# Block-sparse attention and a two-layer MoE in one kernel: V in three prepared layouts, the weight conversion in steps of its own, x in two rings of five

## The chip, the cores and the metric

One core of a Trainium2 chip runs the whole program. It has five engines with a queue of their own: TensorE (PE), VectorE (DVE), ScalarE (ACT), GpSimd (POOL) and SyncE (SP), which here issues every DMA. Each queue runs its instructions strictly in program order, and an instruction that has to wait holds up all that stand behind it. The metric is the device time of one execution in microseconds (us). Before the change it is 1017.01 us, the median of three runs (1015.11 to 1021.48).

## What is computed

```
# attention: batch 4, 8 heads, 768 positions, 64 per head, 24 blocks of 32
scores = (q @ k.T) / sqrt(64)
mask   = |block(i) - block(j)| <= 1, or block i or j is 0 or 23, or j in sampled_blocks[i] (3 per block)
attn   = softmax(where(mask, scores, -1e9));  x = (attn @ v) put together as [3072, 512]
# MoE layer: w_in [512, 2048], w_out [2048, 512]
h = x @ w_in
g = h where h >= 1, 0 where h <= -1, (h + 1)^2 / 4 between
out = g @ w_out
```

The weights arrive as 64-bit floats. The kernel turns them into 32-bit floats with integer operations, and each 32-bit number into a high and a low part, so that three fast matmul passes (high-high, high-low, low-high) give the wanted precision.

## The kernel before

**Attention** is done in pairs: a pair is one batch entry `b` (0 to 3) and two heads (`j`, 0 to 3). A pair goes through four rounds of query blocks: round 0 is the global blocks against all keys, rounds 1 to 3 take 6, 8 and 8 of the other 22 blocks. A round is a chain: `scores` (PE, line 298), `top` (row maxima, DVE, line 309), `expo` (ACT, lines 326 and 329), `turn` (transposes on PE, line 335), `turn_copy` (line 339, ACT or DVE), `values` (PE, line 353), `norm` (DVE, lines 376 to 380). After rounds 2 and 3 a half of `x` is transposed (`x_turn`), and stored as high and low part (`x_hi` on ACT, `x_lo` on DVE) in tile `xt`.

Three tiles hold the V rows of a pair. `vn` holds all rows. `va` holds in its four partition quarters, for each block, the block before it, the block itself, the block after it and block 0; `vb` holds the last block and the three sampled blocks. A sampled block is copied from `va` to `vb` on POOL (line 266) or read from memory by a DMA on SP (line 264); `V_SPW` says which of the three go by SP in the first batch entry, `V_SP` in the others. The sampled K columns go to `kg` (line 231), on POOL, and for `k in KD` on DVE in the first batch entry. A pair of the first batch entry is "wide": its rounds 0, 1 and 2 run before any MoE work and use all PSUM banks, and `TCOPYW` and the table `PW` hold for it. Its round 3 comes later, with `va`, `q` and `k` loaded again.

**The MoE layer** has eight stages, one for each half (384 tokens) of each batch entry. A stage goes over 16 slices `fi` of the hidden dimension: `l1` (lines 472 to 474), the activation (ACT and DVE), `l2` (lines 500 to 502). In the first stage w_out is converted on the way, two slices at a time, and kept in memory (`w_keep`); later stages load it back (`w_load`).

**Conversion** (`convert`, lines 156 to 186) comes sixteen times: eight for w_in (conversions 0 to 7, of which 4 to 7 are for the second half of its columns, wanted from slice 8 on) and eight for w_out (8 to 15). One is: `load` of tile `raw` (two DMAs of 512 KB, line 163), `bits` (an Abs on ACT at line 170, then four DVE operations, lines 171 to 176, into tile `cva`), and `split` (a cast to the high part on ACT, line 75 by way of a helper, and a subtraction on DVE, line 182). `raw` and `cva` have one buffer each, so a load can't start until the `bits` of the conversion before are done.

**What sets the order.** Every step is put into a list with a planned time (`at`), worked out from the tables `P`, `PW`, `PD` and from `TP0`, `CONV` and the like. The list is sorted, and the steps are written into the program in that order. Nothing waits for a planned time: it decides only who stands ahead of whom in each queue. On SP each DMA uses one of eight completion counters in turn, so a DMA also waits until the one eight places ahead of it has landed.

The later batch entries are interleaved with the MoE stages. `xt` has six buffers for each of its two halves (`XBUFS`), and `X2`, `X3` shift the second half of the pairs 2 and 3 to a later place.

Of the kernel before, what the change touches and what calls it, by code (L numbers as in the profile page):

```python
# [27 lines left out]
VROWS = S + BLK  # L28
# [13 lines left out]
def body(ctx, tc, qk_t, v_ext, sampled_blocks, moe_w_in, moe_w_out, near, ident, out):  # L42
# [7 lines left out]
    xp = pool("xp", XBUFS)  # L50
# [19 lines left out]
    def f(ap):  # L70
        return ap.bitcast(F32)
# [70 lines left out]
    def plan_conversions():  # L142
        last = 1e9
        todo = []
        for t, *rest in sorted(conv, key=lambda x: -x[0]):
            last = min(t, last - P["cd"])
            todo.append((last, *rest))
        prev = -1e9
        for t, load, bits, split, parts in todo[::-1]:
# [6 lines left out]
    def convert(t, src, parts):  # L156

        st = {}

        def load():  # L160
            st["raw"] = cv.tile([128, 1024, 2], I32, name="raw", bufs=RAWB)
            for k in range(2):
                Q_RAW.dma_start(out=st["raw"][:, k * 512:(k + 1) * 512],
                                in_=src[k].bitcast(I32).rearrange("p (c w) -> p c w", w=2))

        def bits():
            raw = st["raw"]
            lo32, hi32 = raw[:, :, 0], raw[:, :, 1]
            a = st["a"] = cv.tile([128, 1024], I32, name="cva", bufs=CVAB)
            nc.scalar.activation(out=f(a), in_=f(hi32), func=AF.Abs)  # L170
# [8 lines left out]
        def split(cs, dst, done):  # L179
            hi, lo = dst()  # L180
            rounded(CH, hi, f(st["a"][:, cs]))
            nc.vector.tensor_tensor(out=lo, in0=f(st["a"][:, cs]), in1=f(hi), op=ALU.subtract)
            if done:
                done()

        conv.append((t, load, bits, split, parts))


# [12 lines left out]
    def pair(b, j, s, q, wide, rounds=(0, 1, 2, 3)):  # L201
# [44 lines left out]
        def gather_v(r):  # L246
            vb = st["vb", r] = gat.tile([128, 8, VROW], F32, name="vb", bufs=VBUFS)
            for k0, i0, n in runs(r):
                c = 1 if i0 + n == NB - 1 else 0
                Q_V.dma_start(out=vb[0:32, k0:k0 + n - c], in_=rows(S - BLK, BLK, n - c, 0))  # L250
                if c:
                    Q_V.dma_start(out=vb[0:32, k0 + n - 1:k0 + n], in_=rows(S, BLK, 1, 0))

        def gather_v_sampled(r, engine):
            vb = st["vb", r]
            for k0, i0, n in runs(r):
                for k in range(n):
                    for a in range(NR):
# [128 lines left out]
        def x_hi(hf):  # L387
            x = xt[b, j, hf] = xp.tile([128, 2, HALF], F32R, name=f"xt{hf}")
# [11 lines left out]
        for k, r in enumerate(rounds):  # L400
# [25 lines left out]
            if r >= 2:  # L426
                y = y + G["va"] + G["no"] + (0 if b == 0 or r == 2 else (0, 0, X2, X3)[j])
# [4 lines left out]
                else:  # L432
                    wanted.append((y + G["xt"], steps, r - 2))
# [15 lines left out]
    def moe(t0, p, b, hf, first):  # L449
# [41 lines left out]
        def g_lo(fi):  # L491
            gl = g["gl", fi] = mt.tile([128, HALF], F32R, name="gl", bufs=2)
            (nc.gpsimd if first and fi % 4 in GL1 else nc.vector).tensor_tensor(out=gl, in0=g["r", fi], in1=f(g["gh", fi]), op=ALU.subtract)  # L493
# [95 lines left out]
_INS = ["qk_t", "v_ext", "sampled_blocks", "moe_w_in", "moe_w_out"]  # L589
# [15 lines left out]
def _rows(_np, a):  # L605
# [3 lines left out]
    return _np.concatenate([a, _np.zeros((B, NP, BLK, VROW), _np.float32)], axis=2)  # L609
# [30 lines left out]
```

## Time and profile before

| | us |
|---|---|
| median of three runs | 1017.01 |
| the profiled execution, its own time | 1015.81 |
| its span, first to last instruction | 1014.0 |
| PE busy in it | 837.8 |
| DVE, ACT, POOL busy | 435.8, 411.8, 387.0 |

In the views below a row of a timeline gives the start, the length, the engine and what it did ("x12" is twelve instructions merged), and in brackets how long the engine had stood idle and who released it. "SPq" is the queue of SP: its rows are DMA issues, and their length includes what the issue waits for. A row of waits gives the total of a kind of wait, how often, and the longest. The granted clock (PEclk) is a share of the full TensorE clock of 2.4 GHz; 0.5 is the lower level of 1.2 GHz.

### The profile page before, as it was taken

The page shows a single profiled execution, that of the slowest core. Times are in us where ns is not written, and L with a number is a line of the kernel's source. Part 1 is how long each engine was busy: PE and PEld are TensorE (multiplying, and loading weights), DVE is VectorE, ACT ScalarE, POOL GpSimd, SP SyncE. Part 2 cuts the span into 40 slices and gives each one's busy share as a digit, 9 for nine tenths or more (in the row PEclk, how much of TensorE's full clock was granted, in tenths as well). Part 3 has the DMA queues.
Part 4 walks back from the last instruction along what each step waited for, and adds up shares of the span by engine and source line. Part 5 has one row for each costly group of instructions (what it writes and reads, how often), then busy time and mean ns, then how long its engine had stood idle before and what let it go on. Part 6 is the DMA issues. An engine that isn't in the chain of part 4 may idle for free.

```text
span 1014.0 us, 34082 instructions
## 1 busy us (share of the span) xinstructions
PE 837.8 (83%) x12000; PEld 691.2 (68%) x12000; DVE 435.8 (43%) x1013; ACT 411.8 (41%) x812; POOL 387.0 (38%) x1564
## 2 busy tenths in 40 slices
PE   2532634775778899899999999999999999999997
PEld 1321423654666677777888887887777777899996
DVE  6555753553546343444444434344443343322222
ACT  1432432433343443445444544354444343433433
POOL 2011133558265656645454545555453630000000
PEclk9857657997798999999999999999999999999999
DMA  8467658998574674637474757465645732433432
GB/s 187 103 175 165 132 148 173 240 229 221 174 192 118 178 184 131 138 110 188 145 168 138 183 154 167 139 177 147 173 122 170 163 103 96 151 129 125 156 125 94
DMA packets 137599, 157.54 MB, mean 155 GB/s; under 512 B 13779, under 2 KB 108756, under 8 KB 137428
## 3 DMA queue, kind: packets, MB, share of 16 engines
q1 hardware_dynamic: 137428, 155.35, 57.6%
q8 instruction: 96, 1.57, 0.7%
q14 instruction: 75, 0.61, 0.2%
HBM read 140.61 MB, written 14.68 MB: 153 GB/s over the span
## 4 chain that ended last, share of the span: by engine, by line
PE 63%; DVE 13%; DMA 8%; ACT 7%; issue 4%; SPq 3%; DVEq 1%; ACTq 0%
PE oa L500 8%; PE h L472 8%; PE oa L501 7%; PE oa L502 7%; PE h L474 6%; PE h L473 6%; PE o L353 6%; PE s L298 6%; PE t L335 5%; DMA raw<-in_moe_w_out_dram 3%; DVE m L309 3%; DMA raw<-in_moe_w_in_dram 3%; ACT p L329 2%; DVE pt L339 2%; SPq L264 2%
## 5 line engine op out<-in xcount | busy, mean ns | idle before, releaser
L231 POOL COPY kg<-k 128x32 f32 x912 | 178.0, 227 | 283.8 <-PE s L298 195.1
L266 POOL COPY vb<-va 32x130 f32 x648 | 208.8, 326 | 162.5 <-DMA va<-in_v_ext_dram 102.4
L472 PE MATMUL h<-xt,wi 128*128 128x384 f32 x448 | 164.9, 368 | 38.1 <-DVE r L484 26.7
L500 PE MATMUL oa<-w,gh 128*128 128x512 f32 x384 | 163.8, 427 | 0.4 <-ACT gh L75 0.3
L474 PE MATMUL h<-xt,wi 128*128 128x384 f32 x448 | 154.1, 344 | 0.0
L473 PE MATMUL h<-xt,wi 128*128 128x384 f32 x448 | 154.0, 344 | 0.0
L502 PE MATMUL oa<-w,gl 128*128 128x512 f32 x384 | 152.8, 398 | 0.0
L501 PE MATMUL oa<-w,gh 128*128 128x512 f32 x384 | 152.2, 396 | 0.0
L478 ACT ACTIVATE r<-h,half_c 128x384 f32<-128x384 f32 x112 | 65.3, 583 | 164.5 <-PE h L474 164.0
L484 DVE SCALAR_TENSOR_TENSOR r<-r,h 128x384 f32<-128x384 f32 x112 | 61.7, 551 | 146.5 <-ACT r L481 146.3
L472 PEld LDWEIGHTS h<-xt,wi 128*128 128x128 f32 x448 | 86.9, 194 | 52.2 <-DVE r L484 31.5
L335 PE MATMUL t<-idf,p 128*128 128x128 f32 x464 | 78.2, 293 | 42.1 <-ACT p L326 18.5
L335 PEld LDWEIGHTS t<-idf,p 128*128 128x128 f32 x464 | 54.5, 147 | 70.3 <-ACT p L326 27.0
L75 ACT CAST gh<-r 128x384 fp32r<-128x384 f32 x128 | 65.7, 514 | 89.3 <-DVE r L484 88.8
L493 DVE TENSOR_TENSOR gl<-r,gh 128x384 fp32r<-128x384 f32 x128 | 72.3, 565 | 60.1 <-ACT gh L75 59.8
L329 ACT ACTIVATE p<-s,m 128x256 f32<-128x256 f32 x176 | 71.8, 473 | 62.4 <-DVE m L321 53.0
L473 PEld LDWEIGHTS h<-xt,wi 128*128 128x128 f32 x448 | 87.2, 195 | 4.6 <-issue 1.4
L474 PEld LDWEIGHTS h<-xt,wi 128*128 128x128 f32 x448 | 86.5, 193 | 0.0
L500 PEld LDWEIGHTS oa<-w,gh 128*128 128x128 f32 x384 | 72.9, 190 | 17.0 <-issue 3.9
L502 PEld LDWEIGHTS oa<-w,gl 128*128 128x128 f32 x384 | 72.6, 189 | 16.7 <-DVE gl L493 0.3
L298 PE MATMUL s<-k,q 64*32 64x96 f32 (+2 forms) x3376 | 72.8, 267 | 11.6 <-DMA q<-in_qk_t_dram 6.2
L501 PEld LDWEIGHTS oa<-w,gh 128*128 128x128 f32 x384 | 73.3, 191 | 6.6
(87 smaller groups left out, 1132.3 us busy)
## 6 DMA issues: line engine op xcount, KB each, us to landing
w<-wo_dram SPq DMA_DIRECT2D x112, 512.0 KB, 3.4
va<-in_v_ext_dram SPq DMA_DIRECT2D x40, 357.5 KB, 8.2
raw<-in_moe_w_in_dram SPq DMA_DIRECT2D x16, 512.0 KB, 6.2
raw<-in_moe_w_out_dram SPq DMA_DIRECT2D x16, 512.0 KB, 8.4
wo_dram<-w SPq DMA_DIRECT2D x16, 512.0 KB, 5.7
va<-in_v_ext_dram SPq DMA_DIRECT2D x20, 406.2 KB, 5.9
k<-in_qk_t_dram SPq DMA_DIRECT2D x20, 384.0 KB, 5.0
q<-in_qk_t_dram SPq DMA_DIRECT2D x20, 384.0 KB, 4.2
```

What stands on the lines that cost most here:

```text
L231: eng.tensor_copy(out=kg[:, k0 + k, 32 * a:32 * a + 32], in_=kt[:, bass.ds(field(v, a, NB - 1) * BLK, BLK)])
L266: nc.gpsimd.tensor_copy(out=dst, in_=st["va"][32:64, bass.ds(v, 1)].rearrange("p a d -> p (a d)"))
L298: nc.tensor.matmul(out=st["s", r, e][32 * w:32 * w + 32, 256 * g + c0:256 * g + c1], lhsT=st["q"][es, i * BLK:(i + 1) * BLK], rhs=rhs, sta ...
L329: nc.scalar.activation(out=p[:, 256 * g:256 * g + 256], in_=st["s", r, e][:, 256 * g:256 * g + 256], func=AF.Exp, bias=st["m", r][:, e, g: ...
L335: nc.tensor.transpose(out=t[:, c * 128:(c + 1) * 128], in_=st["p", r, e][:, c * 128:(c + 1) * 128], identity=idf)
L472: nc.tensor.matmul(out=hv, lhsT=wi[:, j, 0, fs], rhs=x[:, 0], start=(j == 0), stop=False)
L473: nc.tensor.matmul(out=hv, lhsT=wi[:, j, 0, fs], rhs=x[:, 1], start=False, stop=False)
L474: nc.tensor.matmul(out=hv, lhsT=wi[:, j, 1, fs], rhs=x[:, 0], start=False, stop=(j == NP - 1))
L493: (nc.gpsimd if first and fi % 4 in GL1 else nc.vector).tensor_tensor(out=gl, in0=g["r", fi], in1=f(g["gh", fi]), op=ALU.subtract)
L500: nc.tensor.matmul(out=o, lhsT=gh[:, ts], rhs=w[:, 0], start=(fi == 0), stop=False)
L501: nc.tensor.matmul(out=o, lhsT=gh[:, ts], rhs=w[:, 1], start=False, stop=False)
L502: nc.tensor.matmul(out=o, lhsT=gl[:, ts], rhs=w[:, 0], start=False, stop=(fi == NF - 1))
```

## The change

V comes in three arrays that the host lays out beforehand: `v_rows` for `vn`, `v_near` for `va` (each partition's 25 blocks in one run of 13,000 bytes, with zeros where nothing belongs), and `v_last` for the last block in `vb`. Each of `vn` and `va` becomes one DMA over 128 partitions, and the last block one DMA a round.

```
-            Q_V.dma_start(out=va[32:64], in_=rows(0, BLK, NB + 1, BLK))
-            Q_V.dma_start(out=va[0:32, 1:NB - 1], in_=rows(0, BLK, NI, BLK))
-            Q_V.dma_start(out=va[64:96, 1:NB - 1], in_=rows(2 * BLK, BLK, NI, BLK))
-            Q_V.dma_start(out=va[96:128, 2:NB - 1], in_=rows(0, BLK, NI - 1, 0))
-            Q_V.dma_start(out=va[96:128, 1:2], in_=rows(S, BLK, 1, 0))
+            Q_V.dma_start(out=va, in_=v_near[b, j])
...
-            for k0, i0, n in runs(r):
-                c = 1 if i0 + n == NB - 1 else 0
-                Q_V.dma_start(out=vb[0:32, k0:k0 + n - c], in_=rows(S - BLK, BLK, n - c, 0))
-                if c:
-                    Q_V.dma_start(out=vb[0:32, k0 + n - 1:k0 + n], in_=rows(S, BLK, 1, 0))
+            k = 3 if r == 1 else 0
+            Q_V.dma_start(out=vb[0:32, 0:total], in_=v_last[b, j, :, k:k + total])
```

`bits` is cut into `size` (the Abs) and `bits` (the DVE operations), `split` into `high` and `low`, each with a planned time of its own (`cb`, `cz`), and `cva` has two buffers. All tables are new. In the first batch entry fewer sampled K columns go to DVE and fewer sampled V blocks to SP (both to POOL), and one more `turn_copy` goes from ACT to DVE. `xt` has two rings of five, and a store into it is planned no earlier than about the end of the stage that frees its buffer.

```
-            at(t, bits)
+            at(t, size)
+            at(t + P["cb"], bits)
             for later, *part in parts:
-                at(t + P["cs"] + later, split, *part)
+                at(t + P["cs"] + later, high, *part)
+                at(t + P["cs"] + P["cz"] + later, low, *part)
...
+                    old = (b * NP + j - XB[r - 2]) // NP
+                    free = NP * TP0 + DELAY + (old * 2 + r - 1) * 1.5 * TPM - 4.0 if old >= 0 else 0
+                    wanted.append((max(y + G["xt"], free), steps, r - 2))
...
-KD = (0, 1, 2, 4)
+KD = (0,)
-V_SPW = (0, 1)
+V_SPW = (0,)
-RAWB, CVAB = 1, 1
+RAWB, CVAB = 1, 2
-TCOPYW = (0, 1)
+TCOPYW = (0,)
-XBUFS = 6
+XB = (5, 5)
-CONV, CSTEP = 5.557, 8.518
-CONV1, CSTEP1 = 38.599, 8.708
+CONV, CSTEP = 5.244, 11.074
+CONV1, CSTEP1 = 47.887, 8.285
```

By the tables conversions 4 to 7 stood at the planned times 38.6, 47.3, 56.0 and 64.7 and stand at 47.9, 56.2, 64.5 and 72.7, where the first `l1` is planned at 81.1 before and 82.4 now; conversion 8 goes from 76.4 to 77.4.

In the queue of SP, this is what stood between the sampled blocks of the first pair and those of the second (`va`, `vn` and `vb` are the V tiles, `raw` the weights, `k` and `q` the next pair's inputs):

```order
L240 DMA va<-in_v_ext_dram 32x25x130
L241 DMA va<-in_v_ext_dram 32x22x130
L242 DMA va<-in_v_ext_dram 32x22x130
L243 DMA va<-in_v_ext_dram 32x21x130
L244 DMA va<-in_v_ext_dram 32x130
L163 DMA raw<-in_moe_w_in_dram 128x1024 x2
L207 DMA k<-in_qk_t_dram 128x768
L207 DMA q<-in_qk_t_dram 128x768
L211 DMA vn<-in_v_ext_dram 128x6x130
L250 DMA vb<-in_v_ext_dram 32x3x130
L250 DMA vb<-in_v_ext_dram 32x2x130
L252 DMA vb<-in_v_ext_dram 32x130
```

And this is what stands there in the changed kernel:

```order
L243 DMA va<-in_v_near_dram 128x3250
L214 DMA q<-in_qk_t_dram 128x768
L214 DMA k<-in_qk_t_dram 128x768
L218 DMA vn<-in_v_rows_dram 128x780
L165 DMA raw<-in_moe_w_in_dram 128x1024 x2
L249 DMA vb<-in_v_last_dram 32x780
```

Thirteen DMAs have become seven. In the stretch behind it the sampled blocks of rounds 1 and 2 of a wide pair were 12 and 16 DMAs and are 6 and 8, with one DMA for the last block ahead of the 16 where there were two.

In the queue of ACT, this stood where the last conversion of w_in passes into the first of w_out, just ahead of the first MoE stage (`L170` is the Abs of a conversion, `L75` the cast of one, `pt` a turn copy, `xt` the last half of x that the stage needs, `p` the exponentials of the first round 3):

```order
L329 ACTIVATE p<-oa_1885,m_1934 128x256 x2
L75 CAST wi<-cva 128x1024
L339 COPY pt<-h 128x512
L339 COPY pt<-t 128x512
L170 ACTIVATE cva<-raw 128x1024
L389 CAST xt_2153<-h 128x384
L329 ACTIVATE p<-s,m_2150 128x256 x4
L75 CAST w<-cva 128x512
```

In the changed kernel it is:

```order
L326 ACTIVATE p<-oa_1841,m_1890 128x256 x2
L170 ACTIVATE cva<-raw 128x1024
L336 COPY pt<-h 128x512
L170 ACTIVATE cva<-raw 128x1024
L74 CAST wi<-cva 128x1024
L386 CAST xt_2112<-h 128x384
L326 ACTIVATE p<-s,m_2115 128x256 x4
L74 CAST w<-cva 128x512
```

The Abs of conversion 7 now stands behind the last exponentials of the wide pairs (before, it stood ahead of them), and that of conversion 8 two places behind it, ahead of the cast of conversion 7 and of the last store to `xt`.

## Rows read from the trace of the kernel before

**Rows 1.** The page: the span.

```profile
span 1014.0 us, 34082 instructions
```

**Rows 2.** The windows view in four stretches: up to the first `l1`, up to the first output of the first MoE stage, up to about the end of the attention work, and the rest. Columns: length, busy time of PE, of its weight loads, of DVE, ACT and POOL (instructions in brackets), granted clock, busy share of the DMA engines, GB/s.

```profile
0.00:176.10 176.10, 69.69 (x1741) 50.60 (x1741) 99.80 (x299) 54.22 (x94) 33.03 (x129) 0.73 0.66 155
176.10:342.60 166.50, 125.05 (x1854) 101.47 (x1854) 85.50 (x158) 68.58 (x134) 98.20 (x354) 0.88 0.78 197
342.60:850.00 507.40, 485.24 (x7469) 398.22 (x7470) 205.46 (x474) 223.83 (x461) 255.76 (x1083) 1.00 0.56 151
850.00:1014.00 164.00, 157.81 (x939) 140.92 (x937) 45.05 (x83) 65.20 (x123) 0.00 (x0) 0.99 0.37 127
```

**Rows 3.** Marks of the stages: the timeline of PE with the round-0 scores of pairs 0, 1 and 3 (a group of 32 matmuls each), the view of line 472 with the first and last start of `l1`, and the timeline of SP with the first output.

```profile
6.21 1.96 PE L298 MATMUL s<-k,q 64*32 64x256 f32 x32 [6.21 <-DMA q<-in_qk_t_dram]
...
41.70 1.82 PE L298 MATMUL oa<-k,q 64*32 64x256 f32 x32
...
120.33 1.09 PE L298 MATMUL oa<-k,q 64*32 64x256 f32 x32
...
L472 PE MATMUL h<-xt,wi x448: 332/338/689, 176.1 to 999.1; 128*128 128x384 f32 x150
...
342.62 0.85 SPq L510 DMA_DIRECT2D out_dram<-ot  x2
```

**Rows 4.** The waits view from 0 to 157 us.

```profile
POOL vb L266 <- DMA va<-in_v_ext_dram: 90.7, 5, 31.8
ACT cva L170 <- DMA raw<-in_moe_w_in_dram: 37.0, 5, 13.7
DVE cva L171 <- ACT cva L170: 33.5, 6, 10.7
```

**Rows 5.** The timeline of SP from one load of conversion weights to the next but one, in the third pair.

```profile
86.92 0.83 SPq L163 DMA_DIRECT2D raw<-in_moe_w_in_dram  x2
...
91.01 2.23 SPq L250 DMA_DIRECT2D vb<-in_v_ext_dram  x2
...
94.07 9.73 SPq L264 DMA_DIRECT2D vb<-in_v_ext_dram  x12
103.91 0.83 SPq L163 DMA_DIRECT2D raw<-in_moe_w_in_dram  x2
104.84 0.85 SPq L250 DMA_DIRECT2D vb<-in_v_ext_dram  x2
105.96 10.74 SPq L264 DMA_DIRECT2D vb<-in_v_ext_dram  x16
116.80 0.36 SPq L240 DMA_DIRECT2D va<-in_v_ext_dram  x1
...
120.68 1.72 SPq L244 DMA_DIRECT2D va<-in_v_ext_dram  x1
122.51 0.82 SPq L163 DMA_DIRECT2D raw<-in_moe_w_in_dram  x2
```

**Rows 6.** The view of tile `raw`: the time from a DMA's issue to its landing over all 32 loads (least, median, most). Then single rows of the timelines of ACT and SP: the Abs of conversions 1, 8, 9 and 15, the two issues of the loads for conversions 9 and 10.

```profile
DMA to landing us min/median/max: 3.6/7.0/10.3
...
38.70 1.12 ACT L170 ACTIVATE cva<-raw 128x1024 f32<-128x1024 f32 x1 [2.31 <-DMA vb<-in_v_ext_dram]
...
169.27 1.12 ACT L170 ACTIVATE cva<-raw 128x1024 f32<-128x1024 f32 x1 [11.28 <-DMA raw<-in_moe_w_out_dram]
...
177.19 0.83 SPq L163 DMA_DIRECT2D raw<-in_moe_w_out_dram  x2
...
186.83 1.20 ACT L170 ACTIVATE cva<-raw 128x1024 f32<-128x1024 f32 x1 [0.76 <-DVE w L182]
...
192.06 1.21 SPq L163 DMA_DIRECT2D raw<-in_moe_w_out_dram  x2
...
307.58 1.13 ACT L170 ACTIVATE cva<-raw 128x1024 f32<-128x1024 f32 x1
```

**Rows 7.** The view by line and shape, whole span: busy time and mean ns of the Abs, of the four DVE operations of `bits`, of a turn copy on DVE and of a K copy on DVE.

```profile
L170 ACT ACTIVATE cva<-raw 128x1024 f32<-128x1024 f32 x16 | 18.2, 1138 | 72.3 <-DMA raw<-in_moe_w_in_dram 37.0 <-DMA raw<-in_moe_w_out_dram 29.7 <-DVE w L182 3.3
L171 DVE TENSOR_SCALAR cva<-cva 128x1024 f32<-128x1024 f32 x16 | 11.3, 708 | 66.2 <-ACT cva L170 66.2
L172 DVE TENSOR_SCALAR cva<-cva 128x1024 int32<-128x1024 int32 x16 | 11.2, 699 | 0.5
L174 DVE SCALAR_TENSOR_TENSOR cva<-raw,cva 128x1024 int32<-128x1024 int32 x16 | 19.6, 1228 | 0.5
L176 DVE SCALAR_TENSOR_TENSOR cva<-raw,cva 128x1024 int32<-128x1024 int32 x16 | 19.6, 1227 | 0.6
L339 DVE COPY pt<-t 128x512 f32<-128x512 f32 x52 | 35.9, 691 | 67.8 <-PE t L335 67.8
L231 DVE COPY kg<-k 128x32 f32 x144 | 24.4, 186 | 10.5 <-issue 6.8
```

**Rows 8.** The timeline of POOL: one round of K copies and two rounds of V copies in the first MoE stage.

```profile
175.25 5.01 POOL L231 COPY kg<-k 128x32 f32 x24 [11.07 <-DMA k<-in_qk_t_dram]
180.32 5.63 POOL L266 COPY vb<-va 32x130 f32 x16
...
201.50 8.83 POOL L266 COPY vb<-va 32x130 f32 x16 [1.87 <-DMA va<-in_v_ext_dram]
```

**Rows 9.** The waits view, whole span: the one wait of `l1` for a half of x.

```profile
PE h L472 <- DVE xt L393: 8.5, 1, 8.5
```

More of the change, by code (lines that the diff above doesn't have):

```diff
@@ L41, in body @@
 @with_exitstack
-def body(ctx, tc, qk_t, v_ext, sampled_blocks, moe_w_in, moe_w_out, near, ident, out):
+def body(ctx, tc, qk_t, v_rows, v_near, v_last, sampled_blocks, moe_w_in, moe_w_out, near, ident, out):
     nc = tc.nc
@@ L49, in body @@
     pr = pool("pr", 2)
-    xp = pool("xp", XBUFS)
+    xp = pool("xp", 1)
     mt = pool("mt", 2)
@@ L148, in plan_conversions @@
         prev = -1e9
-        for t, load, bits, split, parts in todo[::-1]:
+        for t, load, size, bits, high, low, parts in todo[::-1]:
             at(max(t - P["cl"], prev + 0.1), load)
             prev = t
-            at(t, bits)
+            at(t, size)
+            at(t + P["cb"], bits)
             for later, *part in parts:
-                at(t + P["cs"] + later, split, *part)
+                at(t + P["cs"] + later, high, *part)
+                at(t + P["cs"] + P["cz"] + later, low, *part)
     def convert(t, src, parts):
+        n = len(conv)
         st = {}
@@ L164, in load, with size @@
                                 in_=src[k].bitcast(I32).rearrange("p (c w) -> p c w", w=2))
+        def size():
+            a = st["a"] = cv.tile([128, 1024], I32, name="cva", bufs=CVAB)
+            nc.scalar.activation(out=f(a), in_=f(st["raw"][:, :, 1]), func=AF.Abs)
         def bits():
-            raw = st["raw"]
+            a, raw = st["a"], st["raw"]
             lo32, hi32 = raw[:, :, 0], raw[:, :, 1]
-            a = st["a"] = cv.tile([128, 1024], I32, name="cva", bufs=CVAB)
-            nc.scalar.activation(out=f(a), in_=f(hi32), func=AF.Abs)
             nc.vector.tensor_scalar(out=f(a), in0=f(a), scalar1=CLO, scalar2=CHI, op0=ALU.max, op1=ALU.min)
@@ L177, in bits, with high, low @@
                                            op0=ALU.logical_shift_right, op1=ALU.bitwise_or)
[L179 to L182, printed above, removed]
+        def high(cs, dst, done):
+            st[cs.start] = dst()
+            rounded(CH, st[cs.start][0], f(st["a"][:, cs]))
+        def low(cs, dst, done):
+            hi, lo = st[cs.start]
+            (nc.gpsimd if n in SUBP else nc.vector).tensor_tensor(out=lo, in0=f(st["a"][:, cs]), in1=f(hi), op=ALU.subtract)
             if done:
                 done()
-        conv.append((t, load, bits, split, parts))
+        conv.append((t, load, size, bits, high, low, parts))
     xt = {}
@@ L492, in g_lo @@
             gl = g["gl", fi] = mt.tile([128, HALF], F32R, name="gl", bufs=2)
-            (nc.gpsimd if first and fi % 4 in GL1 else nc.vector).tensor_tensor(out=gl, in0=g["r", fi], in1=f(g["gh", fi]), op=ALU.subtract)
+            (nc.gpsimd if first and fi in GL1 else nc.vector).tensor_tensor(out=gl, in0=g["r", fi], in1=f(g["gh", fi]), op=ALU.subtract)
         def l2(fi, t):
@@ L608, in _rows @@
     a = a.transpose(0, 1, 3, 2, 4).reshape(B, NP, S, VROW)
-    return _np.concatenate([a, _np.zeros((B, NP, BLK, VROW), _np.float32)], axis=2)
+    rows = a.reshape(B, NP, S // 128, 128, VROW).transpose(0, 1, 3, 2, 4)
+    blocks = a.reshape(B, NP, NB, BLK, VROW).transpose(0, 1, 3, 2, 4)
+    near = _np.zeros((B, NP, 4, BLK, NB + 1, VROW), _np.float32)
+    near[:, :, 0, :, 1:NB - 1] = blocks[:, :, :, 0:NB - 2]
+    near[:, :, 1, :, 0:NB] = blocks
+    near[:, :, 2, :, 1:NB - 1] = blocks[:, :, :, 2:NB]
+    near[:, :, 3, :, 2:NB - 1] = blocks[:, :, :, 0:1]
+    last = _np.zeros((B, NP, BLK, 9, VROW), _np.float32)
+    last[:, :, :, 0:8] = blocks[:, :, :, NB - 1:NB]
+    return rows, near.reshape(B, NP, 128, NB + 1, VROW), last
 def kernel(**inputs):
```

36 lines of the change are left out of this document (16 added, 20 removed).

## Prediction, made before the changed kernel ran

> **What bounds the kernel now.** I read the windows view first, by stages. The span is 1014.0 us [rows 1] and the execution took 1015.81, so 1.8 us lie outside it; the median of the runs is 1.2 above that execution. PE is busy for 69.7 of the first 176.1 us, for 125.1 of the next 166.5, for 485.2 of 507.4 and for 157.8 of the last 164.0 [rows 2]. Its idle time is therefore 106.4, 41.5, 22.2 and 6.2 us: 148 of 176 us lie ahead of 342.6. After that PE has work 96% of the time and the granted clock is 1.00 or 0.99; a change can win little there. So the question is what the first 342.6 us wait for.
>
> Next the marks and the timeline of SP. The wide pairs follow each other every (120.33 - 6.21) / 3 = 38.0 us, the first `l1` comes at 176.1 and the first output at 342.6 [rows 3]. In the third pair one turn of SP's queue, from the load at 86.92 to the next but one at 122.51, takes 35.6 us, about that pitch, and is full from end to end [rows 5]: 28 sampled blocks take 9.73 + 10.74 = 20.5 us (0.73 each), the five DMAs of `va` take from 116.80 to 122.40, which is 5.6 us. SP is the engine that the pairs go at.
>
> The waits say how that reaches the others: POOL stood 90.7 us for `va`, ACT 37.0 us in front of the Abs for `raw`, DVE 33.5 us for that Abs [rows 4]. The last two matter most, since exponentials, maxima and turn copies stand behind them in the same queues, and PE stands behind those. The conversions form one chain, because `raw` has one buffer: issue, landing, Abs, four DVE operations, next issue. Conversion 1 has its Abs at 38.70, conversion 8 at 169.27, conversion 15 at 307.58 [rows 6]: a pitch of 130.6 / 7 = 18.7 us, then of 138.3 / 7 = 19.8 us. The first `l1` follows conversion 8 by 6.8 us and the first output conversion 15 by 35.0 us [rows 3, 6]. So the first stage's end is 38.7 + 7 x 18.7 + 7 x 19.8 + 35.0 = 342.6, and the change is worth what it takes from these four terms.
>
> **SP, per wide pair.** Sampled blocks go from 28 DMAs to 14: 14 x 0.73 = 10.2 us instead of 20.5. `va` goes from five DMAs to one: about a fifth of 5.6, 1.1 us. The last blocks go from five DMAs to two. In the rows the first two took 2.23 and the two of round 2 0.85, so 1 us remains. Two loads of `raw` at 0.83 stay (1.7 us) [rows 5], and `q`, `k` and `vn` are three issues more, 1.2 us at the 0.41 that one of the two of `raw` took. The sum is 15.2 us instead of 35.6. SP stops being the bound as long as a pair takes more than that.
>
> **The conversion chain in the wide pairs.** What remains is the chain itself: 0.83 for two issues, the landing, 1.14 for the Abs and 0.71 + 0.70 + 1.23 + 1.23 = 3.86 for the DVE operations [rows 5, 7], so 5.8 us and the landing. A landing took 3.6 to 10.3 us, 7.0 in the middle [rows 6]. V's many small packets go, the bytes of the weights stay, so I take 6.7, near the median: a pitch of 12.5 us, or 25 us a pair. The high end is the longest landing, 16.1 us. The low end is set by DVE: it is busy 99.8 us in the first stretch [rows 2], loses 24 K copies of 0.186 a pair and gains three turn copies of 0.69 [rows 7], a net -2.4 us a pair, so about 90 us or 22.6 a pair, which is 11.3 us a conversion. I take 12.5: it lies 1.2 above what DVE can do without a wait.
>
> **The start.** The load of conversion 1 stood behind 12 sampled blocks and now behind 6 (4.4 us by 0.73), but the Abs stands behind the exponentials of round 2 in ACT's queue, and round 1 must now wait for twelve K and twelve V copies on POOL. I take 36 us for the Abs of conversion 1 instead of 38.7; bounds 33 and 38.7.
>
> **The first MoE stage.** The fastest turn of the chain there was 9.6 us from issue to Abs (177.19 to 186.83) and 5.2 us from Abs to the next issue (to 192.06), 14.9 in all [rows 6]; the mean was 19.8 because SP was in `va` or sampled blocks when `raw` came free, and because the DMA engines were full. The stretch moved 197 GB/s at a busy share of 0.78, while the last stretch, which has no V, moved 127 at 0.37 [rows 2]. At that second efficiency the same bytes need 197 / (127 / 0.37) = 0.57 of the time, 96 us, instead of 130. V is only a part of the bytes and the sampled blocks stay small, so between 96 and 130 I expect about 105 us of DMA work, in a shorter stage. That leaves the landing still loaded but not queued: I take 14.5 us, just under the fastest turn. The low end is PE: 125.05 us at a clock of 0.88 is 110 us of work at full clock, so conversion 8 to first output is not below 6.8 + 110 = 117 us, against 7 x 14.5 + 35 = 136.5. The high end is halfway from the fastest turn to the mean, 17.3.
>
> **What I cost at nothing.** The 24 K copies and 14 V copies a pair that go to POOL lie beside the chain. A round of POOL copies shows 0.209 us a K copy and 5.63 / 16 = 0.35 a V copy [rows 8], so 30 and 28 of them make 16.1 us of a pair's 25. Without that cover, if POOL reads at the slower of the two rounds shown (8.83 us, 0.55 each), it is 21.7 us, still below 25. The Trainium skill, SBUF — State Buffer, section "Who interferes with whom", says that GpSimd and a VectorE instruction with two SBUF inputs exclude each other for the whole instruction; this speaks against moving copies to POOL in the wide pairs, where most DVE operations of a conversion are of that kind. The two rounds of the same 16 copies, 5.63 and 8.83 us, agree with it; by the first the term is 0, by the second also.
>
> Of the other edits: the second `cva` buffer lets an Abs start ahead of the last subtraction, but `raw` still closes the chain, so 0. Separate times for Abs, cast and subtraction only move them among their neighbours, 0 apart from the pitch above. Conversions 4 to 7 stand some 9 planned units later, yet ahead of conversion 8, so the chain's length is the same; the Abs of 7 and 8 come close together before the first stage, and the 6.8 us behind conversion 8 stay, since the last store to `xt` still follows its Abs. The two rings of five are reused one pair earlier, about one stage before the data is wanted; what hides it is that slack, and if it is gone a wait like the one of 8.5 us [rows 9] comes back at stage ends. After 342.6 I change nothing: PE is the bound, its work is the same, and fewer DMAs on SP can only touch the 28 us of idle time there.
>
> **Sum.** End of the first stage: 36 + 7 x 12.5 + 7 x 14.5 + 35 = 260 us instead of 342.6, that is -2.7, -43 and -37, together -82.6. The span becomes 931.4, the execution 933.2; with the 1.2 us by which the median stands above, 934 us. All low ends: 33 + 7 x 11.3 + 117 = 229, a span of 900. All high ends: 38.7 + 7 x 16.1 + 7 x 17.3 + 35 = 307.5, a span of 979.
>
> **Rivals.** (a) The queues run into each other less than I allow, and DVE and then PE are the bounds: 900 to 915. For it: the fall in DMA count is large. Against: every queue is in order, and 1.2 us of slack a conversion is little. 0.15. (b) The landing stays slow, or POOL becomes the bound of the wide pairs. With all its copies slowed as V was (8.83 / 5.63 = 1.57) it needs 25.3 us a pair, and with a wait for `va` some 30; three pairs later by 5 us and a stage pitch of 17 make 934 + 15 + 17 = 966. 955 to 985, chance 0.22. (c) SP was full but not the cause; the engines wait for each other in a ring, and the pitch stays near 18.7. Against it is that POOL's and ACT's waits end on DMAs, not on each other. Within 1%: 0.04. (d) Slower: with rings of five the stores to `xt` wait at every stage end, PE stands with them, and seven boundaries pay it. At the 8.5 us shown once [rows 9] that is 60 us and the time 994; it outweighs the gain by 1% only from (82.6 + 10) / 7 = 13.2 us a boundary. Against: the halves are planned a stage ahead. 0.04.
>
> **Chances.** My forecast, 915 to 955, has 0.55. Faster by over 1% (1% is about what a measurement of this kernel can tell from no change): 0.55 + 0.15 + 0.22 = 0.92; within 1% 0.04; slower 0.04. The range of 900 to 980 is that of the bounds, and leaves out (c), (d) and the outer part of (b). The likeliest case's own range is 915 to 955.
>
> **What the profile would show.** Right: SP has gaps in the wide pairs; the round-0 scores come some 25 us apart; the first `l1` at about 130, the first output at about 260; the Abs still waits for `raw`, by a few us each; from the first output to the end 671 us as before. Wrong: a pitch near 38 with SP idle (c); POOL's copies without a gap and DVE or PE waiting for them (b); `l1` waiting for `xt` at stage ends (d); a first stage of over 150 us with the Abs waiting for its load, which would mean that the DMA engines, not SP, had set the landing.

## The result, and the profile after

The changed kernel takes 945.12 us, the median of four runs (943.08 to 947.54), against 1018.73 us of the kernel before on the same chip (1015.11 to 1021.48): a ratio of 0.928, interval 0.9241 to 0.932. (The 1017.01 us above is the median of the first three of these four runs of the kernel before.) Two far slower executions, one of `many_long` (997.48 us) and one of `layout_alone` (2635.4 us), are left out of the medians below. The profiled execution took 944.88 us. The page gives its span:

```profile
span 943.1 us, 33817 instructions
```

The windows view in the same four stretches (up to the first `l1`, up to the first output, up to about the end of the attention work, the rest; columns as in [rows 2]):

```profile
0.00:134.10 134.10, 66.20 (x1740) 50.61 (x1740) 91.47 (x215) 48.28 (x82) 88.18 (x300) 0.77 0.60 202
134.10:273.66 139.56, 114.88 (x1751) 93.74 (x1752) 82.95 (x152) 66.45 (x130) 89.97 (x316) 0.94 0.70 241
273.66:780.00 506.34, 489.77 (x7622) 400.51 (x7628) 207.17 (x481) 225.96 (x464) 259.16 (x1100) 1.00 0.46 155
780.00:943.00 163.00, 157.13 (x903) 140.09 (x890) 44.91 (x84) 65.69 (x124) 0.00 (x0) 1.00 0.36 126
```

The first two stretches lost 42.0 and 26.9 us, the last two together 2. The DMA engines carry more a second (202 GB/s where there were 155) at a smaller busy share (0.60 where there was 0.66). PE's idle time in the first two stretches is now 67.9 and 24.7 us, where it was 106.4 and 41.5 [rows 2].

The marks of [rows 3] (round-0 scores of pairs 0 and 3 on PE, the view of the line of `l1`, now 471, and the first output on SP):

```profile
5.99 1.96 PE L295 MATMUL s<-k,q 64*32 64x256 f32 x32 [5.99 <-DMA k<-in_qk_t_dram]
...
86.69 1.09 PE L295 MATMUL oa<-k,q 64*32 64x256 f32 x32
...
L471 PE MATMUL h<-xt,wi x448: 332/338/687, 134.1 to 928.4; 128*128 128x384 f32 x150
...
273.66 0.37 SPq L509 DMA_DIRECT2D out_dram<-ot  x1
```

Wide pairs follow each other every (86.69 - 5.99) / 3 = 26.9 us, where it was 38.0.

The waits from 0 to 157 us, which answer to [rows 4]:

```profile
POOL vb L263 <- DMA vb<-in_v_near_dram: 15.8, 2, 15.1
ACT cva L170 <- DMA raw<-in_moe_w_out_dram: 8.7, 1, 8.7
ACT cva L170 <- DMA raw<-in_moe_w_in_dram: 2.6, 2, 1.6
```

POOL no longer waits for `va` (it was 90.7 us); 15.8 us go to the sampled blocks that SP reads (a wait of 16.6 us at the start stands in both kernels). And the Abs waits 2.6 us for the loads of w_in (it was 37.0), and 8.7 us once for the first load of w_out.

The timeline of SP from one load of conversion weights to the next but one, in the second and third pair, as [rows 5]:

```profile
53.85 1.28 SPq L165 DMA_DIRECT2D raw<-in_moe_w_in_dram  x2
55.23 0.37 SPq L243 DMA_DIRECT2D va<-in_v_near_dram  x1
55.70 0.38 SPq L214 DMA_DIRECT2D q<-in_qk_t_dram  x1
56.17 0.40 SPq L214 DMA_DIRECT2D k<-in_qk_t_dram  x1
57.65 0.33 SPq L218 DMA_DIRECT2D vn<-in_v_rows_dram  x1
58.03 0.70 SPq L249 DMA_DIRECT2D vb<-in_v_last_dram  x1
58.98 10.24 SPq L261 DMA_DIRECT2D vb<-in_v_near_dram  x6
69.88 0.83 SPq L165 DMA_DIRECT2D raw<-in_moe_w_in_dram  x2
70.80 0.38 SPq L249 DMA_DIRECT2D vb<-in_v_last_dram  x1
71.43 5.68 SPq L261 DMA_DIRECT2D vb<-in_v_near_dram  x8
77.22 0.36 SPq L243 DMA_DIRECT2D va<-in_v_near_dram  x1
80.88 0.83 SPq L165 DMA_DIRECT2D raw<-in_moe_w_in_dram  x2
```

The turn takes 27.0 us instead of 35.6, with gaps. But six sampled blocks that stand soon after a `va` took 10.24 us; by the waits of SP's queue 5.6 of them are one wait, of the fourth block for the `va` eight places ahead of it. The eight sampled blocks that have no `va` that close ahead took 5.68 us, 0.71 each.

Rows of tile `raw`, of ACT (the Abs of conversions 1, 8, 10, 11 and 15) and of SP (loads of `raw` and sampled blocks in the first MoE stage), as [rows 6]:

```profile
DMA to landing us min/median/max: 3.6/5.7/10.2
...
34.30 1.17 ACT L170 ACTIVATE cva<-raw 128x1024 f32<-128x1024 f32 x1
...
126.17 1.12 ACT L170 ACTIVATE cva<-raw 128x1024 f32<-128x1024 f32 x1 [8.66 <-DMA raw<-in_moe_w_out_dram]
...
155.05 1.13 ACT L170 ACTIVATE cva<-raw 128x1024 f32<-128x1024 f32 x1
...
172.40 1.13 ACT L170 ACTIVATE cva<-raw 128x1024 f32<-128x1024 f32 x1 [4.37 <-DMA raw<-in_moe_w_out_dram]
...
240.43 1.15 ACT L170 ACTIVATE cva<-raw 128x1024 f32<-128x1024 f32 x1 [0.96 <-DMA raw<-in_moe_w_out_dram]
...
149.88 10.87 SPq L261 DMA_DIRECT2D vb<-in_v_near_dram  x8
164.35 0.98 SPq L165 DMA_DIRECT2D raw<-in_moe_w_out_dram  x2
...
167.88 13.11 SPq L261 DMA_DIRECT2D vb<-in_v_near_dram  x8
...
182.03 1.24 SPq L165 DMA_DIRECT2D raw<-in_moe_w_out_dram  x2
```

The pitch of the conversions is (126.17 - 34.30) / 7 = 13.1 us in the wide pairs and (240.43 - 126.17) / 7 = 16.3 in the first stage. From an Abs to the next load it is 9.3 and 9.6 us here (155.05 to 164.35, 172.40 to 182.03), where 5.2 would do: SP stood in the eight sampled blocks. The view of the waits of SP's queue over the whole span gives the releaser:

```profile
SPq L261 <- DMA va<-in_v_near_dram: 41.5, 12, 5.6
```

The sampled blocks (line 261) wait for the landing of `va`, up to 5.6 us at a time; 21.9 of the 41.5 us, in five waits, lie ahead of the first output. `va` is now one DMA of 1,625 KB, and it holds one of the eight completion counters until it is all there.

### The profile page after: what moved, and what is told of

It reads as the page before. It is cut to its first block, busy times and chain, and to the rows that moved or that the text cites. A ratio compares the mean times of both kernels' runs of the same rounds, so it can differ in the third digit from the quotient of the medians.

```text
span 943.1 us, 33817 instructions
## 1 busy us (share of the span) xinstructions
PE 828.0 (88%) x12000; PEld 685.0 (73%) x12000; DVE 426.5 (45%) x929; ACT 406.4 (43%) x800; POOL 437.3 (46%) x1716
## 3 DMA queue, kind: packets, MB, share of 16 engines
q1 hardware_dynamic: 56788, 157.40, 48.8%
## 4 chain that ended last, share of the span: by engine, by line
PE 69%; DVE 12%; DMA 7%; ACT 6%; issue 3%; DVEq 1%; POOLq 1%; POOL 1%; SPq 0%; ACTq 0%
PE h L471 9%; PE oa L499 8%; PE oa L501 8%; PE oa L500 8%; PE h L473 7%; PE h L472 7%; PE s L295 6%; PE o L350 6%; PE t L332 5%; DMA raw<-in_moe_w_in_dram 3%; DVE m L306 2%; DMA raw<-in_moe_w_out_dram 2%; DVE pt L336 2%; DVE cva L178 2%; DVE cva L180 1%
## 5 line engine op out<-in xcount | busy, mean ns | idle before, releaser
L238 POOL COPY kg<-k 128x32 f32 x1008 | 205.6, 236 | 238.5 <-PE s L295 171.9
L263 POOL COPY vb<-va 32x130 f32 x704 | 231.5, 329 | 86.6 <-DMA vb<-in_v_near_dram 37.3
L471 PE MATMUL h<-xt,wi 128*128 128x384 f32 x448 | 163.8, 366 | 16.1 <-DVE xt L390 8.4
L471 PEld LDWEIGHTS h<-xt,wi 128*128 128x128 f32 x448 | 85.1, 190 | 33.3 <-DVE r L483 14.0
L472 PEld LDWEIGHTS h<-xt,wi 128*128 128x128 f32 x448 | 85.6, 191 | 3.0
L473 PEld LDWEIGHTS h<-xt,wi 128*128 128x128 f32 x448 | 85.2, 190 | 0.0
L501 PEld LDWEIGHTS oa<-w,gl 128*128 128x128 f32 x384 | 72.4, 188 | 16.6 <-DVE gl L492 0.3
```

What stands on the lines that cost most here:

```text
L238: eng.tensor_copy(out=kg[:, k0 + k, 32 * a:32 * a + 32], in_=kt[:, bass.ds(field(v, a, NB - 1) * BLK, BLK)])
L471: nc.tensor.matmul(out=hv, lhsT=wi[:, j, 0, fs], rhs=x[:, 0], start=(j == 0), stop=False)
L472: nc.tensor.matmul(out=hv, lhsT=wi[:, j, 0, fs], rhs=x[:, 1], start=False, stop=False)
L473: nc.tensor.matmul(out=hv, lhsT=wi[:, j, 1, fs], rhs=x[:, 0], start=False, stop=(j == NP - 1))
L501: nc.tensor.matmul(out=o, lhsT=gl[:, ts], rhs=w[:, 0], start=False, stop=(fi == NF - 1))
```

## The experiments

Each ratio is to runs of the kernel before on the same chip. The chips differ a little: beside `sp_sampled` and the runs named `many_long`, `few_short` and `many_short` the kernel before took 1021.01 us, beside the last four of the table 1016.52, beside the others 1017.25. So where a run is set against one of another group, the difference that the ratios give stands in brackets behind that of the times. Three questions: which part of the change brings the 74 us, whether it is the number of V's DMAs or something else about them, and why the first stage's pitch stayed above the forecast. All fourteen kernels, with the four terms of the prediction's sum read from their traces (Abs of conversion 1, the two pitches, last Abs to first output) and the ratio to the kernel before:

| run | us | ratio (interval) | Abs 1 | wide pitch | stage pitch | tail | first output |
|---|---|---|---|---|---|---|---|
| before | 1018.73 | | 38.7 | 18.7 | 19.8 | 35.0 | 342.6 |
| after | 945.12 | 0.928 (0.9241 to 0.932) | 34.3 | 13.1 | 16.3 | 33.2 | 273.7 |
| layout_alone | 962.53 | 0.9492 (0.9461 to 0.9523) | 36.5 | 15.0 | 17.0 | 31.4 | 291.5 |
| moves_alone | 981.51 | 0.9651 (0.9616 to 0.9685) | 34.5 | 14.9 | 19.8 | 35.9 | 313.2 |
| layout_moves | 947.71 | 0.9322 (0.9291 to 0.9353) | 30.0 | 13.7 | 17.2 | 31.3 | 278.1 |
| sp_sampled | 971.02 | 0.9507 (0.9466 to 0.9548) | 36.0 | 16.5 | 16.9 | 34.3 | 304.2 |
| many_long | 982.41 | 0.9641 (0.9597 to 0.9686) | 34.3 | 15.3 | 18.4 | 35.1 | 305.4 |
| few_short | 954.75 | 0.9349 (0.9312 to 0.9386) | 34.4 | 13.8 | 17.0 | 34.3 | 284.4 |
| many_short | 996.77 | 0.9756 (0.9708 to 0.9805) | 34.4 | 16.2 | 19.8 | 37.0 | 322.8 |
| many_wide | 951.86 | 0.938 (0.9342 to 0.9418) | 34.4 | 13.2 | 16.9 | 32.7 | 277.5 |
| r3_pool | 941.60 | 0.9253 (0.9227 to 0.928) | 34.3 | 12.9 | 15.8 | 35.5 | 270.6 |
| va_early | 952.24 | 0.9362 (0.9344 to 0.9379) | 34.6 | 14.4 | 16.5 | 35.5 | 286.2 |
| r3_pool_va | 948.25 | 0.934 (0.9321 to 0.9359) | 34.3 | 14.1 | 15.3 | 33.6 | 273.3 |
| wide_pool | 951.71 | 0.9362 (0.9337 to 0.9386) | 35.7 | 13.6 | 16.6 | 35.3 | 282.3 |

**Number or shape of V's DMAs.** `many_long` takes the changed kernel and loads `va` by partition quarters again:

```
-            Q_V.dma_start(out=va, in_=v_near[b, j])
+            for q in range(3):
+                Q_V.dma_start(out=va[32 * q:32 * q + 32], in_=v_near[b, j][32 * q:32 * q + 32])
+            for c0, c1 in ((0, 12), (12, NB + 1)):
+                Q_V.dma_start(out=va[96:128, c0:c1], in_=v_near[b, j][96:128, c0:c1])
```

and cuts the DMA for the last block in three or two.

> The changed kernel with its long runs, but with as many V DMAs as before: va in five, the last block in three or two a round. Theory (the number of DMAs on SP is what counted): 7 more DMAs a wide pair at 0.4 to 1.1 us bring SP from about 15 to 20 us a pair, still under the 27 us that a pair now takes, so the wide pairs lose a few us; in the first MoE stage, where SP stands between a free raw tile and the next load, 5 more a round make the conversion pitch longer by about 1 us. 955 to 965 us. Rival (the size of the packets is what counted): as the changed kernel, 943 to 948 us.

`few_short` keeps one DMA each, but the arrays in memory have the block outermost, so that a run is 520 bytes:

```
-            Q_V.dma_start(out=va, in_=v_near[b, j])
+            Q_V.dma_start(out=va, in_=v_near[b, j].rearrange("c p d -> p c d"))
```

> The changed kernel with its few V DMAs, but with V stored so that every run is 520 bytes again. Theory (number of DMAs): 945 to 952 us, with the first l1 near 134 and the first output near 274. Rival (size of the packets): the DMA engines get back about 25 us of work in the first MoE stage and 25 in the wide pairs; loads of raw land later by 2 to 3 us, seven of them in each half: 965 to 980 us.

`many_short` has both edits.

> The changed kernel with both undone: many V DMAs and runs of 520 bytes. What is left of the change is the moved copies, the tables, the second cva buffer and the rings. Theory (number of DMAs) and rival (size of packets) both: the sum of the two other runs, 965 to 985 us. A third reading (the moved copies and the tables alone brought it): 945 to 950 us.

Against 945 the runs stand at +37 (37), +10 (7) and +52 us (48): the DMAs cost most, the runs' length little (the intervals of `few_short` and of the changed kernel just overlap), and both together bring back the pitch of 19.8 in the first stage. But `many_long` changed two things, the count of DMAs and the partitions that each spans. So `many_wide` also has five DMAs for `va`, cut by blocks, each over all 128 partitions (2,600 bytes a run; the last block cut as in `many_long`):

```
-            Q_V.dma_start(out=va, in_=v_near[b, j])
+            for c0 in range(0, NB + 1, 5):
+                Q_V.dma_start(out=va[:, c0:c0 + 5], in_=v_near[b, j, :, c0:c0 + 5])
```

> As the run with many DMAs and long runs (983 us), with the five DMAs of va cut the other way: each over all 128 partitions and five blocks (2,600 bytes a run) instead of over 32 partitions. The last block stays in three or two DMAs. Theory (the number of DMAs in SP's queue and its eight completion counters cost the 38 us): 975 to 990 us, as there. Rival (DMAs over 32 partitions are slow in themselves; the busy share of the DMA engines rose from 0.60 to 0.70 there): 950 to 962 us, with a share near 0.60 in the wide pairs.

It stands at +7 (10), so the count of DMAs, on which the 955 to 965 us expected of `many_long` rested, explains 7 to 10 of the 37. The windows view of the first 134.1 us, the row of SP's queue in the DMA view (packets, MB, share) and its rows of issues (how many, KB each, median us to landing), of `many_long`:

```profile
0.00:134.10 134.10, 64.44 (x1609) 48.52 (x1609) 81.18 (x201) 45.98 (x79) 84.08 (x276) 0.75 0.70 186
...
q1 hardware_dynamic: 61780, 157.41, 55.7%
...
raw<-in_moe_w_in_dram SPq DMA_DIRECT2D x16, 512.0 KB, 8.4
raw<-in_moe_w_out_dram SPq DMA_DIRECT2D x16, 512.0 KB, 5.4
```

and of `many_wide`:

```profile
0.00:134.10 134.10, 65.93 (x1740) 50.06 (x1740) 90.52 (x213) 48.17 (x82) 91.33 (x300) 0.77 0.61 200
...
q1 hardware_dynamic: 71380, 157.41, 50.7%
...
raw<-in_moe_w_in_dram SPq DMA_DIRECT2D x16, 512.0 KB, 5.6
raw<-in_moe_w_out_dram SPq DMA_DIRECT2D x16, 512.0 KB, 5.3
```

Both move 157.41 MB, with five DMAs for each `va`. Those over 32 partitions keep the DMA engines busier (0.70 against 0.61) for fewer bytes a second (186 against 200 GB/s), in fewer packets, and the weights of w_in that share the engines land in 8.4 us instead of 5.6; those of w_out, which come later, land as soon in both (5.4 and 5.3). So 31 (27) of the 37 us belong to the partitions that a DMA spans, not to the number of DMAs. The Trainium skill, DMA: Bandwidth & Descriptors, section "Rules for kernel authors", says of transfers to separate partition halves that they gain nothing beside each other, and that one transfer over 128 partitions is to be used. With quarters in place of halves, these runs agree.

Where the price falls shows from turn to turn. From `many_wide` to `many_long` the seven wide turns together grow by 14.4 us, 8.9 of them from issue to Abs and 5.5 from Abs to the next issue. The seven of the first stage grow by 11.2 us, all but 0.1 from Abs to the next issue, which is SP's part: up to 280 us its queue waits 34.2 us for `va` in `many_long` and 12.0 in `many_wide`. So the narrow DMAs cost most by what stands behind them in the issuing queue, and less by loads that land later.

**Which part brings what.** `layout_alone` is the kernel before with the three V arrays and their DMAs, and nothing else.

> The kernel before with the three V layouts alone: one DMA for va, for vn and for the last block; its tables, its moved copies and its single cva buffer as before. Theory: SP's turn per wide pair falls from 35.6 to about 28 us and the pairs follow it (38 to 30 us apart); in the first MoE stage the load of raw is issued sooner and lands sooner: first l1 near 150, 965 to 985 us. Rival (the moved copies did the wide pairs, and the first stage needs the new tables): 995 to 1010 us.

`moves_alone` is the kernel before with three numbers changed:

```
-KD = (0, 1, 2, 4)
+KD = (0,)
-V_SPW = (0, 1)
+V_SPW = (0,)
-TCOPYW = (0, 1)
+TCOPYW = (0,)
```

> The kernel before with the moved work alone: in the wide pairs one sampled V block of three by SP instead of two, three of four K copies of DVE on POOL, one turn copy on DVE. Theory: SP's turn falls by 14 x 0.73 = 10 us to about 25, the wide pairs end 25 to 35 us sooner; the first MoE stage has nothing of it: 985 to 995 us. Rival (va, not the sampled blocks, holds the pairs): 1005 to 1020 us.

`layout_moves` has both, with the tables, one `cva` and `XBUFS` of before.

> The kernel before with the V layouts and the moved work, but its tables, one cva buffer and one x ring of six as before. Theory (SP is the whole story): 945 to 955 us. Rival (the separate times of the conversion steps and the new tables bring a good part): 960 us or more.

The layout alone brings some 53 us, the moves alone 36, both 70, which is less than the sum: both shorten the same wide turns. The moves help only in the wide pairs (pitch 14.9, but 19.8 in the first stage as before); the layout helps in both. Together they come within 3 us (4) of the whole change, less than the intervals resolve: beside the new layout, tables, separate step times, second `cva` and two rings bring nothing that could be measured. Beside V in many DMAs with short runs that isn't so. `many_short` has the moves and all of these and stands at 0.9756; `moves_alone` has the moves without them and stands at 0.9651, some 11 us better, and the two intervals don't touch. Whether the tables cost that or the fuller `va` of `many_short` (100 blocks over its four quarters, where the kernel before loads 91), no run separates.

`sp_sampled` is the changed kernel with the three numbers of `moves_alone` set back.

> The changed kernel, but in the wide pairs two of three sampled V blocks go by SP again, the K copies of four places go to DVE and both turn copies to ACT. Theory (SP's turn per wide pair set the pace): 14 more DMAs of 0.73 us make SP's turn about 25 us, as long as a pair, and raw loads wait behind them: first l1 at 145 to 155 instead of 134, 955 to 965 us. Rival (the layout alone brought the gain in the wide pairs): first l1 within 3 us of 134, 943 to 949 us.

It costs 26 us (23), where 10 to 20 were expected. The timeline of SP there, one turn of two loads of `raw`:

```profile
67.12 0.83 SPq L165 DMA_DIRECT2D raw<-in_moe_w_in_dram  x2
...
70.89 14.13 SPq L261 DMA_DIRECT2D vb<-in_v_near_dram  x12
85.13 0.83 SPq L165 DMA_DIRECT2D raw<-in_moe_w_in_dram  x2
86.69 11.18 SPq L261 DMA_DIRECT2D vb<-in_v_near_dram  x16
...
98.45 0.85 SPq L165 DMA_DIRECT2D raw<-in_moe_w_in_dram  x2
```

The two groups take 25.3 of the turn's 31.3 us, and with the issues around them SP is busy for 30.0, full almost as in [rows 5]. The wide turns account for 7 x (16.5 - 13.1) = 24 us, and 18 of these lie from Abs to the next issue, where SP's queue stands. That points to the sampled blocks; but `sp_sampled` and `moves_alone` each set three numbers, and no run separates the sampled blocks from the K copies and the turn copy.

**Why the first stage's pitch is 16.3.** `r3_pool` takes the sampled blocks of round 3 in the first batch entry off SP:

```
-                        if (a in (V_SPW if wide else V_SP)) is not (engine is ENG.SP):
+                        if (a in (V_SPW if wide else () if rounds == (3,) else V_SP)) is not (engine is ENG.SP):
```

> The changed kernel, but in the first MoE stage (round 3 of the first batch entry) no sampled V block is read by a DMA on SP: the eight of each of the four groups go to POOL, which copies all 24. Theory (the conversion's next load stands in SP's queue behind sampled blocks, which themselves wait for the one DMA of va to land): three of the seven turns from Abs to the next issue of raw took 9.3, 9.6 and 11.7 us instead of 5.2, 15 us too many; without those DMAs the pitch of conversions 8 to 15 goes from 16.3 to about 14.2, the first output from 273.7 to about 259, the time to 929 to 934. Rival 1 (the landings set the pitch, since the DMA engines are busy 0.70 there): the pitch stays at 16, the time at 942 to 947. Rival 2 (POOL comes late: it is busy 90 of 139.6 us in the stage and gets 32 copies of 0.35 to 0.55, 11 to 18 us more): values and with them PE wait for vb, 950 or more.

The loads of `raw` for conversions 11, 12 and 15, from SP's timeline, the last with the sampled blocks ahead of it:

```profile
162.47 1.52 SPq L165 DMA_DIRECT2D raw<-in_moe_w_out_dram  x2
177.34 0.81 SPq L165 DMA_DIRECT2D raw<-in_moe_w_out_dram  x2
...
218.93 9.10 SPq L261 DMA_DIRECT2D vb<-in_v_near_dram  x8
228.15 0.86 SPq L165 DMA_DIRECT2D raw<-in_moe_w_out_dram  x2
```

The Abs ahead of the first two came at 156.16 and 170.64, so those turns fell from 9.3 and 9.6 us to 6.3 and 6.7: the mechanism is there. The third, behind the Abs at 217.12, still took 11.0; the sampled blocks ahead of it are the next batch entry's, which the edit leaves on SP. Over the six turns that begin with the Abs at 141 us, 6.8 us went from Abs to the next issue, and 1.9 came back from issue to Abs. The pitch fell by 0.5 and not by 2, the tail grew by 2.3 us, and the time is 941.6 where 929 to 934 were expected: below 945, but the intervals overlap.

`va_early` plans `va` for round 3 seven units earlier (`'la': 13.806` becomes `21.0` in `PD`), so that the sampled blocks stand further behind it.

> The changed kernel, but the second load of va in the first batch entry (for round 3) is planned 7 units earlier, so that the sampled blocks of round 3 stand further behind it. Theory (the sampled blocks are slow because they wait for that DMA): the groups of eight, which took 8.3 to 13.1 us, fall to about 6, and the turns that they held up by 4 to 6 us are held up by 1 to 3; the time goes to 934 to 940. Rival 1 (the landings set the pitch): 942 to 947. Rival 2 (va has two buffers, and an earlier load waits for one of them at the head of SP's queue, with raw behind it): 947 to 960.

The first three groups of sampled blocks took 4.83, 7.17 and 9.44 us instead of 8.31, 10.87 and 13.11. But the load for conversion 8 now stands behind `va` (SP's timeline, then ACT's):

```profile
123.21 0.36 SPq L243 DMA_DIRECT2D va<-in_v_near_dram  x1
...
124.64 1.33 SPq L165 DMA_DIRECT2D raw<-in_moe_w_out_dram  x2
...
135.08 1.12 ACT L170 ACTIVATE cva<-raw 128x1024 f32<-128x1024 f32 x1 [17.03 <-DMA raw<-in_moe_w_out_dram]
```

From that issue to the Abs it is 10.4 us, where after the change it was 4.9 (121.23 to 126.17). The time, +7 us (8), lies in the range of rival 2, but not for its reason: SP did not stand at `va`, whose issue took 0.36 us; the load behind it landed late. That `va`, with `q` and `k` now issued right behind it, took the DMA engines is the likely cause: from 123 to 135 us they were busy for 0.78 of the time, where after the change it was 0.58 from 121 to 126.2. `r3_pool_va` has both edits.

> Both edits: no sampled V block of round 3 on SP in the first MoE stage, and va for round 3 planned 7 units earlier. Theory (SP's queue is what lengthens the turn from Abs to the next load): no better than the sampled blocks on POOL alone, 928 to 934, since with no sampled block on SP it doesn't matter to raw when va lands. If POOL waits for va with the first edit alone, this run is the faster of the two by the length of that wait, some 2 to 5 us. Rival (landings set the pitch): 942 to 947.

Its pitch in the first stage is 15.3, the shortest of all, and conversion 8 is late by 6.6 us (Abs at 132.80) for the same reason. The time, +3 us (6), misses the 928 to 934 that were expected: the one gain doesn't pay for the other loss.

**Is SP still the bound of the wide pairs?** `wide_pool` takes their last sampled blocks off SP: `V_SPW = (0,)` becomes `()`.

> The changed kernel, but in the wide pairs no sampled V block is read by a DMA on SP; POOL copies all 42 of a pair. Theory (SP has gaps in the wide pairs, and their pitch of 26.9 us is that of two turns of the conversion chain: issue, landing, Abs and four DVE operations): the pitch stays within 1 us, the time at 940 to 947. Rival 1 (the 14 sampled blocks, 10 us of SP a pair, still hold up the loads of raw): the pitch falls to about 24 and the time to 933 to 938. Rival 2 (POOL becomes the bound: 30 K copies of 0.209 and 42 V copies of 0.35 to 0.55 are 21 to 29 us a pair and it waits for va besides): pitch of 28 to 32, time 950 to 965.

The timeline of POOL there:

```profile
51.45 5.91 POOL L238 COPY kg<-k 128x32 f32 x18
57.42 10.04 POOL L263 COPY vb<-va 32x130 f32 x24
67.53 3.77 POOL L238 COPY kg<-k 128x32 f32 x12
71.36 7.07 POOL L263 COPY vb<-va 32x130 f32 x18
78.49 6.10 POOL L238 COPY kg<-k 128x32 f32 x18
```

POOL has no gap from 51.45 to 84.59, and the values on PE wait 11.6 us for its copies, 10 times, up to 157 us. The round-0 scores of pairs 0 and 3 start at 5.97 and 90.07, so the pairs stand 28.0 us apart, not 26.9. From Abs to the next load it is 5.2 to 5.4 us four times running, so SP holds nothing up there (the fifth time it is 7.0), and yet the time is 7 us (8) longer than 945. With no DMA for sampled blocks on SP, POOL is by these rows the bound of the wide pairs. They and the start make half of the 8.6 us by which the first output is later; the rest lies in the first stage and the tail, which the edit leaves alone, and is not explained.

## Why the prediction was right, and where its sum was off

**The sum.** The span came out at 943.1 us where 931.4 was forecast, 11.7 more. Term by term: the Abs of conversion 1 at 34.3 (36 forecast, -1.7); 7 x 13.12 (7 x 12.5, +4.4); 7 x 16.32 = 114.3 (7 x 14.5 = 101.5, +12.8); last Abs to first output 33.2 (35, -1.8); the rest 669.4 (671.4, -2.0). The mechanism held: the first 342.6 us are one chain of conversions, each term shrank, and what comes behind did not change. The mis-sized term is the first stage's pitch.

**That step.** The 14.5 was "just under the fastest turn": 9.6 us from issue to Abs, 5.2 from Abs to issue. The landing was better than that: from issue to Abs the six turns from 147.03 on took 8.7 us in the mean, where 14.5 left it 9.3, and this hid some 4 us of the miss. From Abs to issue three of six took 9.3, 9.6 and 11.7, together 15 us too many, which is more than the whole 12.8. The step named the sampled blocks on SP as a cause before, and then let them go, although they keep their number in this stage. `r3_pool` shows that they are part of the cause (two turns shorter by 3 us each); it doesn't show the whole, since the time fell by 3.5 us (3), within the intervals, and not by 12 to 15.

**SP, per wide pair.** 15.2 us were forecast; the rows of the turn shown above make 20.95. The miss is one group of six, 10.24 us instead of 4.4, behind a `va` still under way. From issue to Abs a wide turn took 7.1 us in the mean (7.5 forecast), from Abs to issue 6.0 (5.0): two of the seven turns took 8.8 and 7.0 there, the others 5.2 to 5.3. That makes 13.1.

**V's DMAs.** On SP, `va` was put at 1.1 us, a fifth of what its five DMAs took, and its issue took 0.37. But counting DMAs was the wrong measure: five over all partitions cost 7 us in all (10), five over quarters 37. The other worry, many small packets, is worth 10 (7).

**Costed at nothing.** POOL's copies were put at 16.1 us a pair, 21.7 at worst. In the third pair the 28 V copies took 4.00 + 7.97 us, 0.43 each, between the two rates of [rows 8]; with 30 K copies of 0.209 that is 18 us of 26.9, hidden (scores on PE wait for POOL's K copies only in the first pair, 5.5 us). `wide_pool`, with 14 more copies a pair, shows that the cover ends close by. The second `cva`, the step times and the rings at 0: `layout_moves` bears it out within 3 us (4).

**The rivals.** (a) DVE as the bound: no, 91.5 of 134.1 us, and the pitch is above 11.3. (b) In part: the landing did not stay slow, but the first stage took 16.3 a turn where this rival had 17. (c) did not come: pitch and SP's turn went together in the changed kernel and in `sp_sampled`. (d) did not come: `l1` waits for `xt` once, 8.4 us, as it did before [rows 9].

**Open.** Why the tail gave back 2.3 us in `r3_pool` was not settled. The rest of the first stage's excess sits in part in the one turn behind the next batch entry's sampled blocks (11.0 us from Abs to issue where 5.2 would do), and no run takes those off SP. Deeper rings and a second `raw` buffer weren't tried.

## What to carry to other kernels

Look for the chain that closes through a single buffer, and count for each of its turns what stands ahead of its load in the issuing queue, in every stage and not only in the one that the change touches. Load a tile by DMAs that span all partitions; how many there are matters far less, and the price of narrow ones is paid by what stands behind them in the issuing queue and by the other loads on the same engines. A big load moved earlier in a queue is not free either: the next load behind it lands later.

## What the runs showed of the hardware that was not expected

With the same 157.41 MB in all and five DMAs for each `va`, DMAs over 32 partitions held the DMA engines at 0.70 in the first 134.1 us, over 128 partitions at 0.61, and 512 KB loads of w_in took 8.4 us to land against 5.6. Runs of 520 bytes instead of 13,000 made 138,196 packets where there were 56,788, and cost 10 us (7) of 945. A group of six small DMAs soon behind one of 1,625 KB took 10.24 us on SP, 5.6 of them in one wait for its landing; eight with no such DMA close ahead took 5.68. A 512 KB load issued 1.4 us behind such a DMA, with two of 384 KB between, reached its Abs after 10.4 us instead of 4.9.
